# Linear-attention and SwiGLU block: the first chunk's q held in fp32 until its bias is known, and part of the norm sums moved

## The chip, the cores and the metric

The program runs on one core of one Trainium2 chip. The metric is the device time of one execution in microseconds. TensorE multiplies matrices, VectorE and ScalarE work on elements, GpSimd does a few small ones, SyncE (SP) issues the DMAs. [...]

## The reference

All arrays are bf16; x is 2048 rows of 1024.

```python
mod = (silu(c) @ w_mod).reshape(6, 1024)      # sa, ca, ga, sb, cb, gb
h = layernorm(x) * (1 + ca) + sa
q, k, v = split(h @ wqkv)                     # 32 heads of 32
phi = lambda t: where(t > 0, t + 1, exp(t)) + 1e-6
o = phi(q) @ (phi(k).T @ v) / (phi(q) @ sum(phi(k)) + 1e-6)
x = x + ga * (o @ wo)
h = layernorm(x) * (1 + cb) + sb
x = x + gb * ((silu(h @ w_gate) * (h @ w_up)) @ w_down)
```

The change touches the first half alone: the layernorm of x, h, q and k. q of a row needs the shift `sa` only as a constant vector, since (h_scaled + sa) @ wq = h_scaled @ wq + sa @ wq. The kernel uses this for the first 512 rows: it multiplies the scaled rows while `sa` is still being loaded, and adds the bias sa @ wq afterwards.

## The kernel before

**Stages.** The rows are worked in four chunks of 512. For chunk 0, a q phase and then a k phase; for chunks 1 to 3, eight k groups and then eight q groups each (`chunk`, line 837). One group is eight products of a 128x128 weight with 512 rows, accumulated in one PSUM bank over the eight 128-wide pieces of the input (dt 0 to 7). After chunk 3 come the products of phi(k) with the normalised x (`g_group`), the output projection, and the SwiGLU part, which fills the last three quarters of the span.

**Layernorm.** Each of the sixteen 128-row tiles of `XRES` (called x0 to x15 here) gets its sums, on VectorE with BATCH_NORM_STATS (`ln1_stats_ops`) or on ScalarE with two passes that accumulate (`act_stats`, line 574); GpSimd takes the power -0.5; the tile is normalised in place (`ln1_xn`), and SP issues a transposing DMA into `HT` (`th_dma`). `HT` has two halves, for even and odd chunks. There `th_mod` multiplies with 1 + ca and adds sa, per dt. For chunk 0, TensorE transposes instead, and the scaling and the shift are separate (`h0_scale_only`, `h0_shift`).

**q phase of chunk 0** (`q_phase_chunk0`, line 745). Seven groups run side by side in seven banks, two dt at a time, as the weights `wq` arrive. In between stand the products of silu(c) with w_mod for ca and sa (`mod_sc`: 128x128 weights, one column each, into bank 0) and `bias_mm`, 48 products of one column that give the bias into bank 0, columns 16 to 23. The eighth group uses bank 0 after that. Then phi of q is taken from PSUM with the bias (`q_phi`).

**phi** (`phi_evac`, line 654). ScalarE takes exp from the bank into one of four buffers `E1` (for q also relu into `RL`). Of each pair of groups VectorE then takes two TENSOR_SCALAR (min and add) and two final ones (`phi_flush`): for k a SCALAR_TENSOR_TENSOR that reads the bank again, for q a TENSOR_TENSOR of `RL` and `E1`. A k bank is thus free after VectorE's second instruction, a q bank after ScalarE's relu.

**Order.** Every engine runs its instructions in the order in which the program writes them, and a dependency is a semaphore wait; a bank is handed over when the last instruction on it has ended. What stands between the groups is given by dictionaries keyed by the group's number (`kside` for chunk 0's k phase, `s1`, `s2`, `s3` for chunks 1 to 3): the functions of an entry are issued behind that group's products and phi. The bank of a group comes from `next_bank` (line 692): a fixed list of eight, in turn, up to group 40, then five in turn. SP's queue is in order too: loads and transposes that wait for data hold back what is behind them.

**Loads at the start** (lines 397 to 431): x0 to x3, ca, wq, sa, x4 and x5, the first half of wk, x6 and x7, the other half of wk, x8 to x11. The loads of x12 to x15 are issued after chunk 0's q phase (line 830), behind the four transposes of x4 to x7.

**Places of memory that matter.** `WV` (weights of v) and, in the changed kernel, `QPRE` lie at the same 16 KB. `STG` takes 2 MB pieces of w_mod, which VectorE sums with silu(c) (`macc`, eight of 1024 columns for a piece, then `macc_split` and a transpose). `z_row` writes and reads back the sums of phi(k) over SP's queue (`ZB`), `wo_load` brings the output weights, `den` gives the denominators, which go through memory to `RB`.

Of the kernel before, what the change touches and what calls it, by code (L numbers as in the profile page):

```python
# [5 lines left out]
FP32 = mybir.dt.float32  # L6
# [256 lines left out]
def bass_adaLN_cond__linear_attn_block__swiglu_ffn__prompt_kernel(  # L263
# [22 lines left out]
    with ExitStack() as es:  # L286
# [52 lines left out]
        HT = T("ht", 120 * KB, [128, 2, NDT, 512], BF16)  # L339
        WO = T("wo", 120 * KB, [128, NHG, D], BF16)  # L340
# [63 lines left out]
        def sa_load(p):  # L404
            P.dma("wsa%d" % p, WSA[:, :, 512 * p:512 * p + 512], wmv[:, :, 512 * p:512 * p + 512])
# [9 lines left out]
        sa_load(1)  # L415
# [3 lines left out]
        for j in range(2):  # L419
            P.dma("x1_%d" % j, XRES[:, 4 + j, :], xv[:, 4 + j, :])  # L420
        for i in (1, 0):
            P.dma("wk0%d" % i, WQK[:, 4 * i:4 * i + 4, 1024:1536], wqkvv[:, 4 * i:4 * i + 4, 1024:1536])
        for j in range(2, 4):
            P.dma("x1_%d" % j, XRES[:, 4 + j, :], xv[:, 4 + j, :])
# [68 lines left out]
        def th_mod(ch, dt):  # L493
            buf = ch % 2
            if dt % 2 == 0 or ch == 1:
                P.dve("tensor_scalar", out=HT[:, buf, dt, :], in0=HT[:, buf, dt, :], scalar1=MODCOL[:, 0, dt:dt + 1],
                      scalar2=MODCOL[:, 1, dt:dt + 1], op0=ALU.mult, op1=ALU.add)
            else:
                P.act("activation", out=HT[:, buf, dt, :], in_=HT[:, buf, dt, :], func=ACT.Identity,
                      scale=MODCOL[:, 0, dt:dt + 1], bias=MODCOL[:, 1, dt:dt + 1])  # L500
# [23 lines left out]
        def h0_shift(dt):  # L524
            P.dve("tensor_scalar", out=HT[:, 0, dt, :], in0=HT[:, 0, dt, :], scalar1=MODCOL[:, 1, dt:dt + 1],
                  scalar2=None, op0=ALU.add)

        def bias_mm(dts):
            for nt in range(NDT):
                for dt in dts:  # L530
                    P.pe("matmul", out=PS[:, 0, 16 + nt:17 + nt], lhsT=WQK[:, dt, nt * 128:(nt + 1) * 128],
                         rhs=MODTMP[:, dt:dt + 1], start=False, stop=(dt == 3), skip_group_check=True)

        def bias_fin():
            P.dve("tensor_copy", out=BIASQ[:], in_=PS[:, 0, 16:24])
# [17 lines left out]

        def h0_scale(dt):
            P.dve("tensor_scalar", out=HT[:, 0, dt, :], in0=HT[:, 1, dt, :], scalar1=MODCOL[:, 0, dt:dt + 1],
                  scalar2=MODCOL[:, 1, dt:dt + 1], op0=ALU.mult, op1=ALU.add)
# [17 lines left out]
        def act_stats(st, c0=0, mid=None):  # L574
            n = (D - c0) // 512
            junk0 = HT[:, 1, 0:2, :] if st < 8 else JUNK1
# [77 lines left out]
        def phi_evac(bank, dst, bias=0.0):  # L654
            i = phi_ctr[0] % 4
            phi_ctr[0] += 1
            P.act("activation", out=E1[:, i, :], in_=PS[:, bank, :], func=ACT.Exp, bias=bias)
            if not isinstance(dst, tuple):
                P.act("activation", out=RL[:, i, :], in_=PS[:, bank, :], func=ACT.Relu, bias=bias)
            phi_pend.append((i, dst, bank))  # L660
            if len(phi_pend) == 2:
                phi_flush()
# [29 lines left out]
        def next_bank():  # L692
            i = qk_ctr[0]
            qk_ctr[0] += 1
            return (1, 2, 3, 4, 6, 7, 5, 0)[i % 8] if i < 40 else i % 5 + 1

        def q_group(ch, nt):
            buf, bank = ch % 2, next_bank()
            for dt in range(NDT):
                P.pe("matmul", out=PS[:, bank, :], lhsT=WQK[:, dt, nt * 128:(nt + 1) * 128],  # L700
                     rhs=HT[:, buf, dt, :], start=(dt == 0), stop=(dt == NDT - 1))
            phi_evac(bank, PQT[:, nt, ch * 512:(ch + 1) * 512])

        def k_group(ch, nt):
            buf, bank = ch % 2, next_bank()
            for i, dt in enumerate((6, 7, 4, 5, 0, 1, 2, 3) if ch == 0 else range(NDT)):
                P.pe("matmul", out=PS[:, bank, :], lhsT=WQK[:, dt, D + nt * 128:D + (nt + 1) * 128],
                     rhs=HT[:, buf, dt, :], start=(i == 0), stop=(i == 7))
            phi_evac(bank, (ch, nt))
# [35 lines left out]
        def q_phase_chunk0(side):  # L745
# [15 lines left out]
            for nt in range(7):  # L761
                if nt == 4:
                    mod_sc(WSA, 0, range(6, 8))
                    fin_sa(6, 2)
                    for dt in (6, 7):
                        h0_scale(dt)
                q_part(nt, qb[nt], (4, 5))
            mod_sc(WSA, 0, range(4, 6))
            fin_sa(4, 2, True)
            for nt in range(7):  # L770
                if nt == 2:
                    bias_mm((4, 5))
                q_part(nt, qb[nt], (6,))
            for nt in range(7):
                if nt == 1:
                    mod_sc(WSA, 0, range(4))
                    fin_sa(0, 4, True)
                    ln_ops[1][0]()
                    ln_ops[1][1]()
                if nt == 4:  # L780
                    bias_mm(range(4))
                    bias_fin()
                q_part(nt, qb[nt], (7,))
            ln_ops[1][2]()
            ln1_rstd1(5)
# [3 lines left out]
            q_phi = lambda nt: phi_evac(qb[nt] if nt < 7 else 0, PQT[:, nt, 0:512], bias=BIASQ[:, nt:nt + 1])  # L789
            for i, dt in enumerate((4, 5, 0, 1, 2, 3, 6, 7)):  # L790
                P.pe("matmul", out=PS[:, 0, :], lhsT=WQK[:, dt, 896:1024], rhs=HT[:, 0, dt, :], start=(i == 0),
                     stop=(i == 7))
            for dt in (4, 5):
                h0_shift(dt)
            ln1_xn(5)
            th_dma(5)
            for dt in range(4):
                h0_shift(dt)
            ln1_xn(4)
            th_dma(4)  # L800
            for nt in range(8):
                q_phi(nt)
                for f in side.get(nt, []):
                    f()
# [5 lines left out]
        qside, kside = {}, {}  # L810
        ln_ops = [ln1_stats_ops(4 + jj) for jj in range(4)]

        def ln_x1(jj):
            for f in ln_ops[jj]:
                f()
            ln1_rstd1(4 + jj)
        for f in ln_ops[2]:
            add(qside, 1, f)
        for f in ln_ops[3]:
            add(qside, 1, f)  # L820
        add(qside, 1, lambda: ln1_rstd2(6))
        for jj in range(2, 4):
            add(qside, 3, lambda jj=jj: ln1_xn(4 + jj))
            add(qside, 3, lambda jj=jj: th_dma(4 + jj))
# [68 lines left out]
        s3.setdefault(2, []).extend([mod_red, mod_row_a])  # L893
# [321 lines left out]
```

## Time and profile before

| | |
|---|---|
| runs | 828.52, 828.58, 829.11 us (median 828.58) |
| profiled execution | span 827.0 us from the first to the last instruction; the median of the runs is 1.6 us above it |
| TensorE busy | 817.0 us (99%) |
| VectorE, ScalarE busy | 310.8 us (38%), 197.3 us (24%) |
| VectorE busy in 50 to 60, 90 to 100, 120 to 130 us | 9.76, 9.97, 9.86 of 10 |
| chunk 0's k phase begins | 30.41 us |
| chunk 1 begins | 44.21 us |
| last transpose for chunk 1 | landed at 42.97 us |

The span is the time from the first to the last instruction on the chip. A page and a timeline name a group of instructions by line, engine, operation and tile: output tile <- input tiles, shape, count. Nearly all instructions have line 176, a helper's; the tiles tell them apart. In a timeline, the first two columns are start and length in us, and square brackets give the idle time of the engine before the instruction and what ended it. PE is TensorE, PEld its weight loads, DVE VectorE, ACT ScalarE, POOL GpSimd, SPq the DMA queue of SyncE. Matmuls are pipelined: a product of 512 columns lasts 379 ns, and the next one starts 0.216 us after it. Single starts and landings that no view prints are from the trace's records of instructions and semaphores.

### The profile page before, as it was taken

Reading aid. Unit: us, or ns where it says so; the run is one execution under the profiler, and the core shown is the slowest. Engines: PE = TensorE matmul, PEld = TensorE weight load, DVE = VectorE, ACT = ScalarE, POOL = GpSimd, SP = SyncE. Lnnn points to the kernel's source line nnn. Section 1 sums busy time; section 2 is a strip of 40 time slices with the busy share of each in tenths; the row PEclk is TensorE's granted clock in tenths of the full one; section 3 lists DMA queues with packets and bytes.
Section 4 is the critical chain, followed back from the end, with each engine's and each line's share of the span. In section 5 each row is a group of like instructions: output and inputs, shape, how many; then the busy total and the mean of one; then the engine's idle time right before and its main releaser. Section 6 shows DMA issues by size and latency. Waiting matters only on the chain.

```text
span 827.0 us, 10428 instructions
## 1 busy us (share of the span) xinstructions
PE 817.0 (99%) x4244; PEld 376.1 (45%) x4323; DVE 310.8 (38%) x664; ACT 197.3 (24%) x336; POOL 40.7 (5%) x59
## 2 busy tenths in 40 slices
PE   8999999999999999999999999999999999999998
PEld 4544444444444444444444444444444444444444
DVE  5798988476945521111221112122111211221111
ACT  4658643123241111011111101111110111111011
POOL 1010000000130000030000003000000300000000
PEclk9999999999999999999999999999999999999999
DMA  9969665856697995700455570045557004553000
GB/s 317 283 151 225 156 169 144 185 166 200 164 256 234 289 256 153 175 27 23 133 149 152 154 177 29 20 128 153 152 153 185 26 19 124 153 153 87 0 26 26
DMA packets 199360, 119.32 MB, mean 144 GB/s; under 512 B 57992, under 2 KB 183056, under 8 KB 199312
## 3 DMA queue, kind: packets, MB, share of 16 engines
q1 hardware_dynamic: 199296, 118.65, 53.7%
q8 instruction: 34, 0.56, 0.3%
q14 instruction: 14, 0.11, 0.0%
q10 hardware_dynamic: 16, 0.00, 0.0%
HBM read 100.67 MB, written 4.33 MB: 127 GB/s over the span
## 4 chain that ended last, share of the span: by engine, by line
PE 95%; DMA 2%; DVE 1%; SPq 1%; issue 1%; ACT 0%; DVEq 0%; ACTq 0%
PE ps L176 95%; DMA wsa<-in_w_mod_dram 2%; DVE acc L176 1%; SPq L176 1%; DVE pkt L176 0%; DVE e L176 0%; DVE pqt L176 0%; ACT e L176 0%; DVE xres L176 0%; DVE ht L176 0%; DVEq L247 0%; ACTq L247 0%
## 5 line engine op out<-in xcount | busy, mean ns | idle before, releaser
L176 PE MATMUL ps<-h2t,gug 128*128 128x512 bf16 x878 | 210.1, 379 | 0.9
L176 PE MATMUL ps<-h2t,guu 128*128 128x512 bf16 x878 | 209.9, 379 | 0.9
L176 DVE TENSOR_TENSOR at<-sg,ps 128x512 bf16<-128x512 bf16 x112 | 77.0, 688 | 282.7 <-PE ps L176 270.5
L176 ACT ACTIVATE sg<-ps 128x512 bf16<-128x512 f32 x112 | 66.9, 597 | 309.7 <-PE ps L176 298.3
L176 PEld LDWEIGHTS ps<-h2t,guu 128*128 128x128 bf16 x896 | 87.7, 98 | 105.7
L176 PEld LDWEIGHTS ps<-h2t,gug 128*128 128x128 bf16 x896 | 87.6, 98 | 105.5
L176 PE MATMUL ps<-wd_a,at 128*128 128x512 bf16 (+1 forms) x502 | 111.9, 377 | 0.5
L176 PE MATMUL ps<-ht,wqk 128*128 128x512 bf16 x499 | 110.5, 379 | 1.0 <-issue 0.2
L176 PE MATMUL ps<-wd_b,at 128*128 128x512 bf16 (+1 forms) x377 | 84.7, 377 | 0.4
L176 PEld LDWEIGHTS ps<-wd_a,at 128*128 128x128 bf16 x512 | 50.1, 98 | 59.7
L176 DVE TENSOR_TENSOR ut<-att,gb_b 128x512 bf16<-128x512 bf16 (+1 forms) x32 | 13.9, 435 | 167.2 <-ACT att L176 167.2
L176 PEld LDWEIGHTS ps<-ht,wqk 128*128 128x128 bf16 x512 | 49.4, 98 | 59.0 <-DVE ht L176 0.7
L176 ACT ACTIVATE att<-ps 128x512 bf16<-128x512 f32 (+1 forms) x32 | 17.4, 591 | 182.1 <-PE ps L176 182.1
L176 PEld LDWEIGHTS ps<-wd_b,at 128*128 128x128 bf16 x384 | 37.5, 98 | 44.7
L176 PE MATMUL ps<-pk,xres 128*128 128x512 bf16 x250 | 55.4, 379 | 0.6 <-issue 0.5
L176 PE MATMUL ps<-mw,pqt 128*128 128x512 bf16 x249 | 55.5, 379 | 0.5 <-issue 0.2
L176 POOL TENSOR_SCALAR h2t<-h2t,modcol 128x512 bf16<-128x512 bf16 x32 | 26.3, 837 | 383.4 <-DMA h2t<-xn 383.4
L176 ACT ACTIVATE e<-ps 128x512 bf16<-128x512 f32 x56 | 33.2, 604 | 31.9 <-PE ps L176 20.2
L176 PEld LDWEIGHTS ps<-mw,pqt 128*128 128x128 bf16 x256 | 24.7, 98 | 30.2 <-issue 0.5
L176 PEld LDWEIGHTS ps<-pk,xres 128*128 128x128 bf16 x256 | 24.7, 98 | 29.9 <-issue 0.9
L176 ACT ACTIVATE junk<-xres 128x1024 bf16<-128x1024 bf16 x24 | 25.4, 1058 | 34.5 <-DVE xres L176 34.2
L176 DVE SCALAR_TENSOR_TENSOR xres<-ps,xres 128x512 bf16<-128x512 f32 x32 | 21.4, 688 | 11.8 <-PE ps L176 11.6
(107 smaller groups left out, 337.9 us busy)
## 6 DMA issues: line engine op xcount, KB each, us to landing
gug<-in_B_w_gate_dram SPq DMA_DIRECT2D x56, 512.0 KB, 4.0
guu<-in_B_w_up_dram SPq DMA_DIRECT2D x56, 512.0 KB, 5.3
xres<-in_A_x_dram SPq DMA_DIRECT2D x20, 256.0 KB, 4.4
rb<-recip_den SPq DMA_DIRECT2D x8, 512.0 KB, 11.5
stgx<-in_w_mod_dram SPq DMA_DIRECT2D x2, 2048.0 KB, 9.7
wd_a<-in_B_w_down_dram SPq DMA_DIRECT2D x4, 1024.0 KB, 7.4
out_dram<-xres SPq DMA_DIRECT2D x31, 128.0 KB, 1.7
xres<-in_A_x_dram SPq DMA_DIRECT2D x3, 1024.0 KB, 7.1
```

Source lines behind the costliest of these rows:

```text
L176: return getattr(e, method)(**kw)
```

## The change

Chunk 0's q is copied from PSUM as fp32 (`QPRE`) without bias; the shift for chunk 0's k goes into a new tile (`HS`), so the scaled rows stay as they are. The bias products move to chunk 1's q groups: behind each product stands one with the same weights, already in the array, and one column (`bias_mm`, issued without a weight load), into bank 0. phi of chunk 0's q is taken from `QPRE` in the k phases of chunks 2 and 3. The transposes and the norm sums around chunk 0 are ordered anew: x5, x7 and x4 behind the q phase, x6 (sums now on ScalarE) behind the second k group; sums of x8 to x11 in chunk 0's k phase, x12 to x15 earlier in chunk 1. `th_mod` of chunk 1 alternates between VectorE and ScalarE. The loads of x4 to x7 go behind wk's first half, `sa`'s halves change places and go behind wq, the `wv` loads go from chunk 2 to the end of chunk 3, and the sums of w_mod (`macc`) start in chunk 1. `next_bank` has new lists for the first 32 groups.

```diff
+        QPRE = T("qpre", 104 * KB, [128, NHG, 512], FP32)
+        HS = T("hs", 144 * KB, [128, NDT, 512], BF16)
...
         wq_load(4, 2)
-        sa_load(1)
         wq_load(6)
         wq_load(7)
         sa_load(0)
-        for j in range(2):
-            P.dma("x1_%d" % j, XRES[:, 4 + j, :], xv[:, 4 + j, :])
-        for i in (1, 0):
+        sa_load(1)
+        for i in range(2):
             P.dma("wk0%d" % i, WQK[:, 4 * i:4 * i + 4, 1024:1536], wqkvv[:, 4 * i:4 * i + 4, 1024:1536])
-        for j in range(2, 4):
+        for j in range(4):
             P.dma("x1_%d" % j, XRES[:, 4 + j, :], xv[:, 4 + j, :])
...
         def th_mod(ch, dt):
             buf = ch % 2
-            if dt % 2 == 0 or ch == 1:
+            if dt % 2 == 0:
...
+        def bias_mm(nt, dt):
+            w, v, o = WQK[:, dt, nt * 128:(nt + 1) * 128], MODTMP[:, dt:dt + 1], PS[:, 0, nt:nt + 1]
+
+            def fn(e):
+                return e.add_instruction(mybir.InstMatmult(
+                    start_tensor_calc=(nt == 0 and dt == 0), stop_tensor_calc=(dt == NDT - 1), tile_size=(128, 128),
+                    tile_position=(0, 0), ldweights=False, bass_skip_group_check=True,
+                    name=nc.get_next_instruction_name(), ins=[e.lower_ap(v), e.lower_ap(w)], outs=[e.lower_ap(o)]))
+
+            P.add("pe", fn, reads=[w, v], writes=[o], tag="matmul")
...
+            if i < 8:
+                return (2, 3, 4, 6, 7, 5, 0, 3)[i]
+            if i < 24:
+                return (1, 2, 3, 4, 6, 7, 5)[(i - 8) % 7]
+            if i < 32:
+                return (3, 4, 6, 7, 1, 2, 5, 0)[i - 24]
             return (1, 2, 3, 4, 6, 7, 5, 0)[i % 8] if i < 40 else i % 5 + 1
...
+                if ch == 1:
+                    bias_mm(nt, dt)
...
+        def q_copy(nt, bank):
+            P.act("activation", out=QPRE[:, nt, :], in_=PS[:, bank, :], func=ACT.Copy)
...
+            for nt in range(7):
+                q_part(nt, qb[nt], (4, 5))
+            for dt in (6, 7):
+                h0_scale_only(dt)
+            for nt in range(7):
+                q_part(nt, qb[nt], (6,))
+            mod_sc(WSA, 0, range(4))
+            fin_sa(0, 4, True)
+            for dt in range(4):
+                h0_shift(dt)
+            for nt in range(7):
+                q_part(nt, qb[nt], (7,))
+                q_copy(nt, qb[nt])
+            mod_sc(WSA, 0, range(4, 8))
+            fin_sa(4, 4, True)
+            q_part(7, qb[0], range(NDT))
+            q_copy(7, qb[0])
+            for dt in range(4, 8):
+                h0_shift(dt)
             act_stats(4)
+            for j in (5, 7):
+                for f in ln_ops[j - 4]:
+                    f()
+                ln1_rstd1(j)
+            ln1_xn(5)
+            th_dma(5)
             for f in act_mv_ops(4):
                 f()
             neg_rstd(4)
+            ln1_xn(7)
+            th_dma(7)
             ln1_xn(4)
             th_dma(4)
...
+        add(kside, 0, lambda: act_stats(6))
+        for f in act_mv_ops(6):
+            add(kside, 1, f)
+        add(kside, 1, lambda: neg_rstd(6))
+        add(kside, 1, lambda: ln1_xn(6))
+        add(kside, 1, lambda: th_dma(6))
         for dt in range(NDT):
-            add(kside, 1, lambda dt=dt: th_mod(1, dt))
-        for jj, k in ((0, 3), (1, 4)):
-            add(kside, k, lambda jj=jj: act_stats(10 + jj))
-        q_phase_chunk0(qside)
+            add(kside, 4, lambda dt=dt: th_mod(1, dt))
+        for jj in range(2):
+            for f in ln1_stats_ops(8 + jj):
+                add(kside, 5 + jj, f)
+            add(kside, 6 + jj, lambda jj=jj: act_stats(10 + jj))
+        add(kside, 6, lambda: ln1_rstd2(8))
+        q_phase_chunk0()
         for st in range(12, 16):
             x_load(st)
         for gi in range(8):
             k_group(0, gi)
...
-            add(s1, 8 + i, lambda i=i: stg_load(i))
-            add(s2, 1 + i, lambda i=i: wv_load(i))
+            add(s1, 3 + i, lambda i=i: stg_load(i))
+            add(s3, 15, lambda i=i: wv_load(i))
...
+        add(s2, 0, bias_fin)
+        for nt in range(8):
+            add(s2 if nt < 4 else s3, 2 * (nt % 4) + 1, lambda nt=nt: phi_evac(None, PQT[:, nt, 0:512], bias=BIASQ[:, nt:nt + 1],
+                                                       src=QPRE[:, nt, :]))
...
-            add(s2, 4 + kt, lambda kt=kt: macc(STG, kt))
-        add(s2, 13, macc_split)
-        add(s2, 13, lambda: P.dma("stg1", STG[:], wmv[:, :, 4096:5120]))
+            add(s1 if kt < 5 else s2, (11, 12, 13, 14, 15, 8, 9, 10)[kt], lambda kt=kt: macc(STG, kt))
+        add(s2, 11, macc_split)
+        add(s2, 11, lambda: P.dma("stg1", STG[:], wmv[:, :, 4096:5120]))
         for kt in range(NDT):
-            add(s3, 4 + kt, lambda kt=kt: macc(STG, kt))
+            add(s3, 6 + kt, lambda kt=kt: macc(STG, kt))
```

More of the change, by code (lines that the diff above doesn't have):

```diff
@@ L524, in h0_shift @@
         def h0_shift(dt):
[L525 to L532, printed above, removed]
+            if dt < 4:
+                P.dve("tensor_scalar", out=HS[:, dt, :], in0=HT[:, 0, dt, :], scalar1=MODCOL[:, 1, dt:dt + 1],
+                      scalar2=None, op0=ALU.add)
+            else:
+                P.dve("tensor_scalar", out=HS[:, dt, :], in0=HT[:, 1, dt, :], scalar1=MODCOL[:, 0, dt:dt + 1],
+                      scalar2=MODCOL[:, 1, dt:dt + 1], op0=ALU.mult, op1=ALU.add)
+        def bias_mm(nt, dt):
[6 more added lines that the diff above has]
+            P.add("pe", fn, reads=[w, v], writes=[o], tag="matmul")
         def bias_fin():
-            P.dve("tensor_copy", out=BIASQ[:], in_=PS[:, 0, 16:24])
+            P.dve("tensor_copy", out=BIASQ[:], in_=PS[:, 0, 0:8])
         def t_view(dt, n=1):
@@ L552, in raw_copy @@
                 P.dve("tensor_copy", out=dst, in_=src)
-        def h0_scale(dt):
-            P.dve("tensor_scalar", out=HT[:, 0, dt, :], in0=HT[:, 1, dt, :], scalar1=MODCOL[:, 0, dt:dt + 1],
-                  scalar2=MODCOL[:, 1, dt:dt + 1], op0=ALU.mult, op1=ALU.add)
         def ln1_rstd1(st):
@@ L575, in act_stats @@
             n = (D - c0) // 512
-            junk0 = HT[:, 1, 0:2, :] if st < 8 else JUNK1
+            junk0 = HT[:, 1, 0:2, :] if st < 6 else JUNK1
             for fn_, sc_, acc_ in ((ACT.Identity, 1.0 / D, SUMX), (ACT.Square, D ** -0.5, SUMSQ)):
@@ L652, in bass_adaLN_cond__linear_attn_block__swiglu_ffn__prompt_kernel, with phi_evac @@
         phi_ctr = [0]
-        def phi_evac(bank, dst, bias=0.0):
+        def phi_evac(bank, dst, bias=0.0, src=None):
             i = phi_ctr[0] % 4
             phi_ctr[0] += 1
-            P.act("activation", out=E1[:, i, :], in_=PS[:, bank, :], func=ACT.Exp, bias=bias)
+            src = PS[:, bank, :] if src is None else src
+            P.act("activation", out=E1[:, i, :], in_=src, func=ACT.Exp, bias=bias)
             if not isinstance(dst, tuple):
-                P.act("activation", out=RL[:, i, :], in_=PS[:, bank, :], func=ACT.Relu, bias=bias)
+                P.act("activation", out=RL[:, i, :], in_=src, func=ACT.Relu, bias=bias)
             phi_pend.append((i, dst, bank))
@@ L701, in q_group @@
                      rhs=HT[:, buf, dt, :], start=(dt == 0), stop=(dt == NDT - 1))
+                if ch == 1:
+                    bias_mm(nt, dt)
             phi_evac(bank, PQT[:, nt, ch * 512:(ch + 1) * 512])
         def k_group(ch, nt):
-            buf, bank = ch % 2, next_bank()
-            for i, dt in enumerate((6, 7, 4, 5, 0, 1, 2, 3) if ch == 0 else range(NDT)):
+            h, bank = HS if ch == 0 else HT[:, ch % 2], next_bank()
+            for dt in range(NDT):
                 P.pe("matmul", out=PS[:, bank, :], lhsT=WQK[:, dt, D + nt * 128:D + (nt + 1) * 128],
-                     rhs=HT[:, buf, dt, :], start=(i == 0), stop=(i == 7))
+                     rhs=h[:, dt, :], start=(dt == 0), stop=(dt == NDT - 1))
             phi_evac(bank, (ch, nt))
@@ L743, in mod_row_b, with q_phase_chunk0 @@
             P.dma("mdr%d" % i, dst[:], MDR[i].unsqueeze(0).to_broadcast([128, D]))
-        def q_phase_chunk0(side):
+        def q_copy(nt, bank):
+            P.act("activation", out=QPRE[:, nt, :], in_=PS[:, bank, :], func=ACT.Copy)
+        def q_phase_chunk0():
             qb = [1, 2, 3, 4, 6, 7, 5]
@@ L759, in q_phase_chunk0 @@
                 q_part(nt, qb[nt], (2, 3))
-            act_stats(4)
[L761 to L785, printed above, removed]
+            for nt in range(7):
[17 more added lines that the diff above has]
+                h0_shift(dt)
+            act_stats(4)
+            for j in (5, 7):
[4 more added lines that the diff above has]
+            th_dma(5)
             for f in act_mv_ops(4):
@@ L788, in q_phase_chunk0 @@
             neg_rstd(4)
[L789 to L798, printed above, removed]
+            ln1_xn(7)
+            th_dma(7)
             ln1_xn(4)
             th_dma(4)
[L801 to L804, printed above, removed]
             qk_ctr[0] = 0
@@ L808, in add @@
             d.setdefault(k, []).append(f)
-        qside, kside = {}, {}
+        kside = {}
         ln_ops = [ln1_stats_ops(4 + jj) for jj in range(4)]
[L813 to L824, printed above, removed]
-        for dt in range(NDT):
-            add(kside, 1, lambda dt=dt: th_mod(1, dt))
-        for jj, k in ((0, 3), (1, 4)):
-            add(kside, k, lambda jj=jj: act_stats(10 + jj))
-        q_phase_chunk0(qside)
+        add(kside, 0, lambda: act_stats(6))
[4 more added lines that the diff above has]
+        add(kside, 1, lambda: th_dma(6))
+        for dt in range(NDT):
+            add(kside, 4, lambda dt=dt: th_mod(1, dt))
[5 more added lines that the diff above has]
+        q_phase_chunk0()
         for st in range(12, 16):
@@ L870, in ln_half @@
                 add(d, k_fin, lambda jj=jj: neg_rstd(st + 2 + jj))
-        ln_half(2, s1, 0, 0, 1)
+        add(s2, 0, bias_fin)
+        for nt in range(8):
+            add(s2 if nt < 4 else s3, 2 * (nt % 4) + 1, lambda nt=nt: phi_evac(None, PQT[:, nt, 0:512], bias=BIASQ[:, nt:nt + 1],
+                                                       src=QPRE[:, nt, :]))
+        for jj in range(2):
+            for f in act_mv_ops(10 + jj):
+                add(s1, 0, f)
+            add(s1, 0, lambda jj=jj: neg_rstd(10 + jj))
         for jj in range(4):
-            add(s1, 2, lambda jj=jj: ln1_xn(8 + jj))
-            add(s1, 2, lambda jj=jj: th_dma(8 + jj))
+            add(s1, 1, lambda jj=jj: ln1_xn(8 + jj))
+            add(s1, 1, lambda jj=jj: th_dma(8 + jj))
         for i, dt in zip([9, 9, 10, 10, 10, 11, 11, 11], range(NDT)):
             add(s1, i, lambda dt=dt: th_mod(2, dt))
-        ln_half(3, s1, 8, 8, 11)
+        ln_half(3, s1, 6, 6, 9)
         for jj in range(4):
-            add(s1, 13 + jj // 2, lambda jj=jj: ln1_xn(12 + jj))
+            add(s1, 10, lambda jj=jj: ln1_xn(12 + jj))
             add(s2, 0, lambda jj=jj: th_dma(12 + jj))
@@ L892, in bass_adaLN_cond__linear_attn_block__swiglu_ffn__prompt_kernel @@
         add(s1, 7, lambda: P.pool("memset", ap=ZHL[:], constant=0.0))
-        s3.setdefault(2, []).extend([mod_red, mod_row_a])
+        s3.setdefault(0, []).extend([mod_red, mod_row_a])
         add(s3, 12, lambda: mod_row_b(7, 0, GA_B))
```

## The prediction

> Names: k0.0 to k0.7 are the eight k groups of chunk 0 (rows 0-511) in order, k1.0 the first of chunk 1, q7 the last q group of chunk 0; HT1 is chunk 1's half of `HT`; x4 is row tile 4 of `XRES`. Times are us from the start of the span.
>
> **What bounds the kernel now.** First the page.
>
> ```profile
> span 827.0 us, 10428 instructions
> PE 817.0 (99%) x4244; PEld 376.1 (45%) x4323; DVE 310.8 (38%) x664; ACT 197.3 (24%) x336; POOL 40.7 (5%) x59
> L176 PE MATMUL ps<-ht,wqk 128*128 128x512 bf16 x499 | 110.5, 379 | 1.0 <-issue 0.2
> ```
>
> TensorE is busy 99% of the span, and its 499 recorded products of the q/k phases waited 1.0 us in all. So no gain can come from a shorter wait on another engine, and each wait that the change adds is paid in full. Second, TensorE's timeline where the change begins.
>
> ```profile
> 19.77 1.46 PE L176 MATMUL ps<-ht,wqk 128*128 128x512 bf16 x6
> 21.41 0.55 PE L176 MATMUL ps<-siluc,wsa 128*128 128x1 bf16 x16 [0.18 <-DMA wsa<-in_w_mod_dram]
> ...
> 24.04 0.55 PE L176 MATMUL ps<-modtmp,wqk 128*128 128x1 bf16 x16
> ...
> 25.78 0.95 PE L176 MATMUL ps<-siluc,wsa 128*128 128x1 bf16 x32
> ...
> 27.24 0.94 PE L176 MATMUL ps<-modtmp,wqk 128*128 128x1 bf16 x32
> 28.04 3.18 PE L176 MATMUL ps<-ht,wqk 128*128 128x512 bf16 x14
> ```
>
> Six products of 512 columns take 1.46 with a last one of 0.379: one per 0.216. Sixteen of one column take 0.55 with a last one of 0.163: one per 0.025, each with its own weight load hidden in that. Third, the timeline around the start of chunk 1, and the answer for the tile `ht`.
>
> ```profile
> 40.78 1.11 ACT L176 ACTIVATE junk<-xres 128x1024 bf16<-128x1024 bf16 x1
> ...
> 43.10 2.67 DVE L176 TENSOR_SCALAR ht<-ht,modcol 128x512 bf16<-128x512 bf16 x8 [1.54 <-DMA ht<-xres]
> ...
> 45.51 0.10 PEld L176 LDWEIGHTS ps<-ht,wqk 128*128 128x128 bf16 x1 [0.23 <-DVE ht L176]
> ...
> 50.57 1.28 DVE L176 BATCH_NORM_STATS2 stats<-xres 128x6 f32<-128x512 bf16 x2
> ```
>
> ```profile
> L176 SPq DMA_TRANSPOSE ht<-xres x12: 1231/1332/3956, 30.3 to 79.2; - x12
> DMA to landing us min/median/max: 3.2/3.4/7.7
> ```
>
> VectorE waits for the last transpose of rows 512-1023 (landed 42.97), scales HT1 in 2.67 (0.33 each), and TensorE, which began chunk 1 at 44.21, already waits about 0.1 for it at 45.5. This is the place with no slack, and the change rewrites it.
>
> **Part by part.**
>
> *Chunk 0's q phase: -1.7.* Before, k0.0 starts at 28.04 + 11 x 0.2157 = 30.41. After, from the eighth product of dt 4 and 5 (starts 20.84, so the next may start at 21.06): 13 products 2.80, 32 one-column products 0.80, 7 products 1.51, 32 more 0.80, q7's 8 products 1.73: k0.0 starts at 28.70. Gone are 48 bias products (1.2) and waits of 0.5. The cover is the loads. `wsa` part 0 now follows `wq` 6 and 7, so it lands about when those did (22.7, wanted at 23.9); `wsa` part 1 ends the same bytes that ended at 25.73 before (wanted at 26.2); the first `wk` piece then lands near 27.2 (wanted at 28.7), the second near 28.7 (wanted at 29.6). Each would cost its lateness. The eight copies of q to fp32 have the PSUM exponentials as nearest rows (0.48 apart on ScalarE) and lie where ScalarE stood idle (14.7 to 26.4).
>
> *Bias products in chunk 1: +1.6.* 64 products of one column, without a weight load, between products of 512. No row has a product without its load; bounds are nothing and 0.039 (the first of a one-column stream), so 0 to 2.5. I take the 0.025 pitch, 1.6.
>
> *Rows 512-1023 reach HT1 later.* x4 to x7 now load behind both `wk` pieces: 29.4, 30.1, 30.8, 31.5 by the same bytes. VectorE: statistics of x5 and x7 (1.64 each with the small ones, as 53.59 to 55.22 shows) 30.1 to 33.4; normalised x5 at 33.9, x7 34.7, x4 35.5. ScalarE: x4's sums 29.4 to 31.65 (two passes, 2.25 to 2.3 as from 40.78), k0.0's exponential, x6's sums to 34.4, k0.1's exponential to 35.0. VectorE flushes k0.0 and k0.1 (two TENSOR_SCALAR of 0.20, two SCALAR_TENSOR_TENSOR of 0.61: 1.62) to 37.1, and normalises x6 at 38.8. On SP's queue the transposes of x5, x7, x4 stand first; before, the second of these was held until the loads of x8 to x11 had landed (36.85), so the third goes at about 36.9. Then the four loads of x12 to x15 (2.4 at 40.02 before), which this change moves ahead of the last transpose, then x6's, at about 40.4. With 0.7 per 256 KB load (their landings before) it lands behind 2.7 us of loads: L = 44.3. Bounds: 43.0 (3.2 after an issue at 39.8) and 46 (a gap like the 1.5 without traffic at 40 to 41.5 before).
>
> *What queues behind that wait: +8.35.* TensorE is at k1.0 at 28.70 + 64 x 0.2157 = 42.5. The scaling of HT1 now alternates: four on VectorE, four on ScalarE (0.705 apart, from the ACTIVATE ht rows at 65 to 71). They stand on ScalarE ahead of the exponentials of k0.5, k0.6, k0.7. So ScalarE: last scaling done L + 2.9; exponential k0.5 to L + 3.5; k0.6; x10's sums 2.3; k0.7's at L + 6.2 to L + 6.8. VectorE: flush of k0.4 and k0.5 L + 3.55 to L + 5.2; statistics of x8 and x9, now queued here (1.44 + 1.64), to L + 8.25; flush of k0.6 and k0.7 to L + 9.95. The new bank list gives k0.7 bank 3, and k1.2 bank 3 again, three groups later (before: eight). TensorE needs it at 42.5 + 16 x 0.2157 = 45.95 and gets it at L + 10 = 54.3: 8.35 late; 7.05 to 10.05 by the bounds. Inside it lies k1.0 waiting for HT1 (done L + 3.3); from L + 5.0 to L + 10 TensorE does nothing. Afterwards the next used banks have long been drained.
>
> *The clock: +1.5.* At the start of the span thirteen warm-up products of 512 columns from 2.61 to 8.3 stand 0.43 apart, later ones 0.216: after rest TensorE ran at half speed for 5.7. No row shows a gap of 5 us later, so: nothing, or half of 5.7 = 2.9. Neither row is nearer (the start is a longer rest, the later gaps of half a microsecond cost nothing): I take 1.5.
>
> [...]
>
> *Chunks 2 and 3: nothing.* Eight phi of q come here: per group two activations (0.57 with a bias operand at 29 to 34) and 0.54 on VectorE (0.20 + 0.335). VectorE was full at 90 to 100 (9.97 of 10) because of the mod sums (1.2 each); five of eight leave chunk 2, so it has 6.5 (k flushes) + 4.3 (q) + 2.15 (phi) + 3.6 (sums) + 1.8 (their split) + 1.3 (scalings) = 19.7 us of work in 27.6. If that cover failed, TensorE would wait on a bank for the excess.
>
> *The `wv` loads behind chunk 3: +0.3.* They stood in chunk 2; now 2 MB lies on SP's queue ahead of `zb`, `wo` and the denominators. 3.9 us of delay reach `rb`; before, VectorE waited 6.0 for it until 161.6, its eighth G evacuation ended at 163.4, and TensorE wanted that at 167.05: 3.6 of cover. Bounds 0 and 2.4.
>
> **Sum**: -1.7 - 0.1 (the wait at 45.5 goes) + 1.6 + 8.35 + 1.5 + 0.3 = +9.95. It is made on a span of 827.0; the runs' median 828.58 has 1.6 around it, which stays. 828.6 + 9.9 = 838.5.
>
> **Rivals.**
> 1. *Early transposes.* L at 41, with x6's transpose overtaking the loads' data: then k1.2 waits to 51.0, 5.05 late, and with the other terms (-0.2, 1.0 for the clock) the time is 834.4. For it: SP's issues alone would allow 39.7. Against: landings came in order of issue. Chance 0.1.
> 2. *No new wait, the other side.* If VectorE drains bank 3 before 45.95, only -1.8 + 1.6 = -0.2 is left: 828.4. For it: before, a like crowd cost 0.1. Against: even with HT1 landed at 38, VectorE alone (flush to 40.35, four scalings 1.3, flush, 3.1 of statistics, flush) ends at 48.2. Chance 0.07; faster by over 0.2% would need free bias products too, 0.03.
> 3. *The bias products don't come at 0.025.* If each one exposes the next weight load (98 ns), 64 cost 6.3: +4.7, 843.2. Against: the 1-column rows hide a load in 0.025. Chance 0.05.
>
> The forecast has 0.75. Its own range is 833.8 (no clock loss, early bound, free products) to 844.6 (all late bounds together); 8 in 10 of everything lies from 831 to 843.5, which takes in rivals 1 and 3 and leaves out the no-wait case and the joint extreme. Within 0.2% (1.66 us, about what a measurement of this kernel tells from no change) 0.07, faster 0.03, slower 0.90.
>
> **What would show it.** k0.0 near 28.7; the last `ht` transpose of chunk 1 landing 43 to 46; ACTIVATE ht between the fifth and sixth exponential of chunk 0; TensorE idle for some 5 us ahead of the third k group of chunk 1, released by DVE pkt; products 0.43 apart after it; 64 one-column products 25 ns long in the pitch. It is wrong if TensorE shows no gap of over 2 us between 42 and 56.

## The result, and the profile after

| | before | after |
|---|---|---|
| runs, median (from to) | 828.77 us (828.52 to 829.11) | 843.79 us (842.70 to 845.29) |
| ratio, 95% interval | | 1.0185 (1.0172 to 1.0197) |
| profiled execution | span 827.0 | span 841.9, time 843.92 |

The changed kernel is 15.0 us slower. The forecast was 838.5, with a range up to 843.5: right in its sign and in its main mechanism, 5.3 too low. One execution of one experiment (x6's transpose first) took 870.02 us at a granted clock of 0.947 and is left out of its median. The page of the changed kernel:

```profile
span 841.9 us, 10483 instructions
...
PE 825.1 (98%) x4339; PEld 375.2 (45%) x4275; DVE 310.5 (37%) x661; ACT 206.2 (24%) x352; POOL 41.2 (5%) x60
...
L176 PE MATMUL ps<-ht,wqk 128*128 128x512 bf16 x448 | 101.7, 383 | 6.3 <-DVE mv L176 4.6
```

The products of the q/k phases now wait 6.3 us (1.0 before), and their mean length rose from 379 to 383 ns, since eight of them stood 0.427 apart instead of 0.216. Where, the timeline of the start of chunk 1 shows:

```profile
43.82 2.93 ACT L176 ACTIVATE ht<-ht,modcol 128x512 bf16<-128x512 bf16 x4 [5.37 <-DMA ht<-xres]
43.84 1.38 DVE L176 TENSOR_SCALAR ht<-ht,modcol 128x512 bf16<-128x512 bf16 x4 [3.93 <-DMA ht<-xres]
...
44.31 4.61 PE L176 MATMUL ps<-ht,wqk 128*128 128x512 bf16 x16 [1.38 <-DVE ht L176]
...
46.65 1.05 ACT L176 ACTIVATE e<-ps 128x512 bf16<-128x512 f32 x2
...
48.69 1.28 DVE L176 BATCH_NORM_STATS2 stats<-xres 128x6 f32<-128x512 bf16 x2
...
50.13 1.23 DVE L176 BATCH_NORM_STATS2 stats<-xres 128x6 f32<-128x512 bf16 x2
...
52.76 0.68 DVE L176 SCALAR_TENSOR_TENSOR pkt<-ps,e 128x512 bf16<-128x512 f32 x1
...
53.50 0.11 PEld L176 LDWEIGHTS ps<-ht,wqk 128*128 128x128 bf16 x2 [5.08 <-DVE pkt L176]
53.50 4.67 PE L176 MATMUL ps<-ht,wqk 128*128 128x512 bf16 x13 [4.58 <-DVE mv L176]
```

This is the chain of the prediction, in its order: x6's transpose lands (L = 43.71), four scalings on each engine, the exponentials behind them on ScalarE, the norm sums of x8 and x9 on VectorE, then the last read of bank 3 (52.76, ended 53.4), and only then k1.2. The last line's "mv" is a neighbour that ended at the same moment; the line above it names the true releaser. Next, the clock, in stretches of 3 us (the columns are the stretch's length, busy time of PE, PEld, DVE, ACT and POOL, granted clock, DMA share, GB/s):

```profile
50.00:53.00 3.00, 0.00 (x0) 0.00 (x0) 2.93 (x10) 2.97 (x6) 0.70 (x1) 1.00 0.00 0
53.70:56.70 3.00, 3.00 (x8) 1.06 (x7) 2.97 (x13) 0.00 (x0) 1.10 (x2) 0.50 0.86 95
60.00:63.00 3.00, 3.00 (x16) 1.35 (x15) 1.29 (x6) 1.19 (x2) 0.00 (x0) 1.00 1.03 194
180.00:183.00 3.00, 2.83 (x105) 1.65 (x106) 3.00 (x6) 0.72 (x1) 0.00 (x0) 0.50 1.03 217
```

TensorE is idle for the whole first stretch, and the granted clock is then 0.50. The fourth stretch is a second slow one that the prediction did not have, in the stage behind chunk 3 (the G stage). Its timeline:

```profile
139.93 1.67 SPq L176 DMA_TRANSPOSE mhlt<-mhl  x1
...
141.64 4.58 SPq L176 DMA_DIRECT2D wv<-in_A_wqkv_dram  x8
...
146.28 0.32 SPq L176 DMA_DIRECT2D z_row<-zr  x1
...
150.63 0.34 SPq L176 DMA_DIRECT2D zb<-z_row  x1
...
155.28 1.33 ACT L176 ACTIVATE gtmp<-zb,modcol 128x512 f32<-128x512 f32 x2 [17.65 <-DMA zb<-z_row]
...
156.85 20.89 PE L176 MATMUL ps<-pk,xres 128*128 128x512 bf16 x96 [1.07 <-DVE g L176]
...
166.26 4.00 SPq L963 DMA_DIRECT2D rb<-recip_den  x8
...
178.14 1.22 DVE L176 TENSOR_TENSOR pqt<-pqt,rb 128x2048 bf16<-128x2048 bf16 x1 [12.22 <-DMA rb<-recip_den]
...
180.17 0.99 PE L176 MATMUL ps<-g,wv 128*32 128x32 bf16 x100 [2.11 <-DVE g L176]
```

The eight `wv` issues hold SP for 4.6; `z_row` lands at 150.6, 0.2 behind the last `wv` data, and only then is `zb` issued. VectorE waits 12.22 for `rb`, and TensorE now waits for G twice. In the kernel before, where chunk 3 ended 9.0 earlier, the same places were:

```profile
130.14 1.64 SPq L176 DMA_TRANSPOSE mhlt<-mhl  x1
131.84 1.15 SPq L176 DMA_DIRECT2D z_row<-zr  x1
134.56 0.33 SPq L176 DMA_DIRECT2D zb<-z_row  x1
...
149.85 4.00 SPq L955 DMA_DIRECT2D rb<-recip_den  x8
...
161.65 1.23 DVE L176 TENSOR_TENSOR pqt<-pqt,rb 128x2048 bf16<-128x2048 bf16 x1 [5.99 <-DMA rb<-recip_den]
```

**The ledger.** From chunk 0's k phase on, TensorE's weight loads come in the same order in both traces. The start of the same weight load, after less before, tells how late TensorE is there; the steps between places are what each part costs. All in us, one profiled execution each; the columns behind the first belong to experiments told below:

| step | changed kernel | wv early | banks | both | all four | wv alone in the kernel before |
|---|---|---|---|---|---|---|
| up to k0.0 (q phase) | -1.46 | -1.28 | -1.68 | -1.94 | -1.97 | -0.20 |
| wait at k1.0 (HT1) | +1.75 | +3.52 | +2.72 | +2.78 | 0 | 0 |
| k1.0 paced by scalings | +0.67 | +1.13 | +0.67 | +0.67 | +0.27 | +0.08 |
| wait at k1.2 (bank 3) | +4.96 | +4.50 | 0 | 0 | 0 | 0 |
| slow clock behind it | +1.49 | +1.49 | 0 | 0 | 0 | 0 |
| bias products | +1.61 | +1.61 | +1.61 | +1.61 | +1.61 | 0 |
| chunks 2, 3, first G groups | 0 | 0 | 0 | 0 | 0 | 0 |
| G stage to its 13th group | +5.09 | 0 | +5.08 | 0 | 0 | +4.10 |
| from there to the SwiGLU part | +0.79 | +0.86 | +0.86 | 0 | +0.85 | +3.44 |
| span, after less before | +14.9 | +11.8 | +9.3 | +3.1 | +0.8 | +7.5 |

The q phase's row holds 0.25 by which this execution's first product of the phase came later; the part itself is -1.70. A weight load that doesn't wait starts one product (0.2) ahead of its own, so the row of a wait holds 0.2 that the next row gives back: the slow clock behind k1.2 costs 1.69 and shows as 1.49. In the column "wv early" k1.0 costs 0.46 more than in the changed kernel; this execution's mean granted clock was 0.994, against 0.996.

### The profile page after: what moved, and what is told of

It reads as the page before. It is cut to its first block, busy times and chain, and to the rows that moved or that the text cites. A ratio compares the mean times of both kernels' runs of the same rounds, so it can differ in the third digit from the quotient of the medians.

```text
span 841.9 us, 10483 instructions
## 1 busy us (share of the span) xinstructions
PE 825.1 (98%) x4339; PEld 375.2 (45%) x4275; DVE 310.5 (37%) x661; ACT 206.2 (24%) x352; POOL 41.2 (5%) x60
## 3 DMA queue, kind: packets, MB, share of 16 engines
HBM read 100.67 MB, written 4.33 MB: 125 GB/s over the span
## 4 chain that ended last, share of the span: by engine, by line
PE 86%; DMA 5%; DVE 5%; ACT 1%; SPq 1%; issue 1%; POOL 0%; ACTq 0%; DVEq 0%
PE ps L176 86%; DVE acc L176 1%; DMA rb<-recip_den 1%; DMA mhlt<-mhl 1%; DMA recip_den<-rcb 1%; DMA wca<-in_w_mod_dram 1%; ACT ht L176 1%; DVE pkt L176 1%; DMA z_row<-zr 1%; DVE red L176 1%; DVE pqt L176 0%; DMA ht<-xres 0%; SPq L913 0%; DVE mhl L176 0%; SPq L176 0%
## 5 line engine op out<-in xcount | busy, mean ns | idle before, releaser
L176 PE MATMUL ps<-ht,wqk 128*128 128x512 bf16 x448 | 101.7, 383 | 6.3 <-DVE mv L176 4.6
L176 PEld LDWEIGHTS ps<-ht,wqk 128*128 128x128 bf16 x448 | 43.3, 98 | 62.7 <-DVE pkt L176 5.1
L176 PE MATMUL ps<-pk,xres 128*128 128x512 bf16 x256 | 57.5, 384 | 1.1 <-DVE g L176 1.1
L176 ACT ACTIVATE junk<-xres 128x1024 bf16<-128x1024 bf16 x26 | 27.4, 1055 | 35.3 <-DVE xres L176 34.9
L176 DVE SCALAR_TENSOR_TENSOR xres<-ps,xres 128x512 bf16<-128x512 f32 x32 | 21.4, 688 | 11.8 <-PE ps L176 11.6
```

The costliest lines, as they stand in the source:

```text
L176: return getattr(e, method)(**kw)
```

## The experiments

**The `wv` loads back in an earlier place**, chunk 3's q groups:

```diff
-            add(s3, 15, lambda i=i: wv_load(i))
+            add(s3, 8 + i // 2, lambda i=i: wv_load(i))
```

> The eight wv loads go from the end of chunk 3 to behind its first four q groups (two at a time), so they are off SP's queue before the transposes and the small write-and-read of the sums of phi(k). Theory A (the wv loads in front of z_row, wo and rb cost the second stage): the waits of the G stage in the changed kernel (1.24 at its sixth group, 2.28 and 1.62 at the first kvt products and behind them, 5.1 in all) go, zb lands some 4 us earlier, the granted clock stays 1.00 there, and the time falls by 5 to 6, to about 838. Rival B (the stage starts late anyway, because VectorE ends chunk 3 late and its transpose of the w_mod sums holds SP): at most 2 of the 5.1 go, about 842. Neither expects a change before chunk 3.

Measured: 839.09 (838.39 to 840.83), ratio 1.0127 (1.0110 to 1.0144). All waits of the G stage are gone (ledger: 5.09 to 0). This execution's L was 45.65, two later than the changed kernel's, so its span saved less than the stage did.

**Another bank list**, in which bank 3 is not handed from k0.7 to a group three places later:

```diff
-                return (2, 3, 4, 6, 7, 5, 0, 3)[i]
+                return (2, 3, 4, 6, 7, 5, 0, 1)[i]
...
-                return (1, 2, 3, 4, 6, 7, 5)[(i - 8) % 7]
+                return (2, 3, 4, 6, 7, 5, 1)[(i - 8) % 7]
...
-                return (3, 4, 6, 7, 1, 2, 5, 0)[i - 24]
+                return (4, 6, 7, 1, 2, 3, 5, 0)[i - 24]
```

> Only the bank lists of the first 32 groups differ: k0.7 goes to bank 1, and chunk 1 starts with banks 2, 3, 4, 6, 7, 5, 1, so that the bank of k0.7 is wanted again at k1.6 and not at k1.2. Theory A (bank 3 wanted back three groups after k0.7, behind ScalarE's scalings and VectorE's statistics, is the wait): the gap of 4.96 at k1.2 and the slow clock behind it (1.5) go, the wait for the scaled rows at k1.0 (2.4) stays, the time falls by 6 to 6.5, to about 837.5. Rival B (VectorE and ScalarE simply have too much to do there, whatever the list): a gap of several us turns up at a later group of chunk 1, and the time falls by less than 3, to 841 or more.

Measured: 839.05 (838.25 to 840.34), ratio 1.0125 (1.0108 to 1.0142). VectorE's and TensorE's timelines of this kernel:

```profile
53.50 0.68 DVE L176 SCALAR_TENSOR_TENSOR pkt<-ps,e 128x512 bf16<-128x512 f32 x1
```

```profile
45.05 11.30 PE L176 MATMUL ps<-ht,wqk 128*128 128x512 bf16 x46 [2.34 <-DVE ht L176]
```

VectorE is still as late with k0.7's bank (54.2), but TensorE goes through without a wait until 56, the next use of that bank, and its 46 products take 11.30: 1.2 more than 45 steps of 0.216, where eight products 0.427 apart would alone add 1.69. The lateness was harmless by itself; the list turned it into a wait.

**Norm sums of x8 to x11 behind the last k group** of chunk 0, where the flush of k0.6 and k0.7 stands ahead of them:

```diff
-                add(kside, 5 + jj, f)
-            add(kside, 6 + jj, lambda jj=jj: act_stats(10 + jj))
-        add(kside, 6, lambda: ln1_rstd2(8))
+                add(kside, 7, f)
+            add(kside, 7, lambda jj=jj: act_stats(10 + jj))
+        add(kside, 7, lambda: ln1_rstd2(8))
```

> The norm sums of x8 to x11 (two on VectorE, two on ScalarE) move from behind k0.5 to k0.7 to behind k0.7 alone, so that the exponential and the flush of k0.7 come before them. Theory A: bank 3 comes free 2.3 + 3.1 us earlier on the two engines, at best 5 earlier; the gap at k1.2 shrinks from 4.96 to 0 to 2, the clock stays 1.00, the time falls by 4 to 6.5, to 837.5 to 840. Rival B (the scaling of chunk 1's rows on ScalarE alone holds the bank): the gap shrinks by less than 1.5 and the time stays above 842.

Measured: 839.46 (839.05 to 839.61), ratio 1.0128 (1.0111 to 1.0145). TensorE's timeline of this kernel:

```profile
44.68 4.61 PE L176 MATMUL ps<-ht,wqk 128*128 128x512 bf16 x16 [1.94 <-DVE ht L176]
50.83 5.14 PE L176 MATMUL ps<-ht,wqk 128*128 128x512 bf16 x23 [1.54 <-DVE pkt L176]
```

The wait at k1.2 falls from 4.96 to 1.91, and behind this shorter wait 23 products take 5.14, 0.216 apart. So 3.05 of the wait are the moved sums.

**All eight scalings of HT1 on VectorE**, as before the change:

```diff
-            if dt % 2 == 0:
+            if dt % 2 == 0 or ch == 1:
```

> All eight scalings of HT1 on VectorE, as in the kernel before, so that ScalarE doesn't wait for L. Theory A (VectorE's own order, scalings, flush, norm sums of x8 and x9, flush, sets when bank 3 is free): VectorE's chain is L + 2.7 scalings + 1.6 + 3.1 + 1.6 = L + 9.0 instead of the measured L + 9.8; k1.2 waits 0.8 less, 843.0. Theory B (the four scalings on ScalarE, ahead of three exponentials, set it): the wait of 4.96 is gone for the most part, 838 to 839.

Measured: 843.05 (841.89 to 845.18), ratio 1.0178 (1.0159 to 1.0197); within the spread of the changed kernel. The wait at k1.2 is 4.17 (0.79 less), and bank 3 comes at L + 9.15, as VectorE's order gives, instead of L + 9.78. Which engine scales hardly matters; VectorE's order does.

**x6's transpose ahead of the loads of x12 to x15:**

```diff
-        for st in range(12, 16):
-            x_load(st)
         for gi in range(8):
             k_group(0, gi)
...
+            if gi == 1:
+                for st in range(12, 16):
+                    x_load(st)
```

> The loads of x12 to x15 stand behind the transpose of x6 instead of ahead of it. Theory A (the four issues and their traffic make L late): the transpose is issued at 38.3, when x6 has its last scaling, and lands 3.3 to 4.1 later, L = 41.6 to 42.4 instead of 43.7; k1.0 waits 0 to 0.5 instead of 1.75; bank 3 still comes about L + 9.8, near 51.8, so the wait at k1.2 stays near 4.7; whole time some 1.5 to 2 shorter, 842. Theory B (the transposes themselves are slow or stalled, whatever stands ahead): L stays at 43.5 to 44.5 and the time at 843.8.

Measured: 842.3 (841.5 to 842.4), ratio 1.0162 (1.0143 to 1.0181). SP's timeline:

```profile
33.97 5.99 SPq L176 DMA_TRANSPOSE ht<-xres  x4
40.01 2.01 SPq L176 DMA_DIRECT2D xres<-in_A_x_dram  x4
```

The transpose landed 3.06 after its issue: L = 41.79, and TensorE didn't wait at k1.0. With the loads ahead it took 4.14 in the changed kernel (39.57 to 43.71) and 4.57 with the `wv` loads early (41.08 to 45.65). The wait at k1.2 stayed, 4.95. This is the prediction's first rival made on purpose, early transposes, and its 5.05 for that wait.

**Seven eighths of the bias products left out** (chunk 0's q then lacks most of its bias):

```diff
-                if ch == 1:
+                if ch == 1 and nt == 0:
```

> Leaves out seven eighths of the bias of chunk 0's q: 8 of the 64 one-column products of chunk 1 remain. Theory A (each costs 0.028 of TensorE's time and nothing else): chunk 1's q phase is 56 x 0.028 = 1.57 shorter, whole time 842.2. Theory B (they slip into the pipeline of the 512-column products): no change, 843.8. Theory C (each exposes the next weight load of 0.098): 5.5 shorter, 838.3.

Measured: 840.74 (840.40 to 844.02), ratio 1.0156 (1.0140 to 1.0172). In the ledger the row of the bias products falls from 1.61 to 0.20: 1.41 for 56 products, 0.025 each, so theory A with the smaller size. The median fell by 3.0, which the products don't explain; its mean granted clock in three of the four runs was 0.998, against 0.996 in half of the changed kernel's, and 0.002 of 842 us is 1.7, what one stretch of 3.413 at half clock costs.

**Twenty products into a free bank in the wait ahead of k1.2**, so that TensorE isn't idle there:

```diff
         def k_group(ch, nt):
+            if ch == 1 and nt == 2:
+                for _ in range(20):
+                    P.pe("matmul", out=PS[:, 4, :], lhsT=IDENT[:], rhs=HS[:, 0, :], start=True, stop=True)
```

> Twenty products of 512 columns whose result nobody reads go into bank 4 ahead of k1.2 (4.3 us of the gap of 4.96), so TensorE isn't at rest there. Theory A (rest halves the clock): k1.2 starts when it did, 53.5, but its eight products stand 0.216 apart and not 0.427, the granted clock stays 1.00 from 50 to 60, and the time falls by 1.5 to 1.7, to about 842.2. Rival B (the slow products come from something else, such as a contended bank): they stay 0.427 apart and the time stays the same.

Measured: 846.96 (843.98 to 848.48), ratio 1.0214 (1.0190 to 1.0239): a miss in the whole, a hit in its place. k1.2 started as late as ever (53.51), and its products then stood 0.216 apart and not 0.427: 1.69 saved. But the G stage cost more, with a wait of 2.38 that no tile explains (2.21 <-issue in its row), and slow products behind it (16 in 5.23 at 185.97, against 3.63). The granted clock of the three longer runs was 0.996, 0.994 and 0.994, that of the profiled one 0.998: by an estimate from 3.413 at half clock, one to two slow stretches of 1.7 more, at places that no trace shows. The next two runs are about the wait.

**The same with the `wv` loads early** (the first and the last edit together).

> 20 products that write to a free bank stand in the wait ahead of k1.2, as in an earlier run, now with the wv loads in chunk 3, where the G stage has no waits. Theory A (they only keep the clock up, and the higher time of the earlier run came from the G stage): 839.1 less 1.5 to 1.7 of slow clock, 837.5. Theory B (the products themselves cost time, wherever): 841 or more.

Measured: 838.82 (838.18 to 839.24), ratio 1.0123 (1.0108 to 1.0138): between the two theories, 0.3 under early `wv` loads alone. The first products recorded behind the wait ahead of k1.2 stand 0.22 apart (5 in 1.25, from 54.93). TensorE's timeline in the G stage:

```profile
180.93 0.43 PE L176 MATMUL ps<-wo,kvt 32*32 32x512 bf16 x15
182.39 0.37 PE L176 MATMUL ps<-wo,kvt 32*32 32x512 bf16 x1 [1.03 <-issue]
```

A wait of 1.03 that no tile explains ("issue"). The twenty products alone have one of 2.21 in this stage, the `wv` loads alone in the kernel before one of 1.69. The page has a queue of instruction packets, 34 with 0.56 MB in the span. The wait ended 2.6 after one of 16 KB began, as the expectation of the next run has it; whose instructions a packet holds, no row tells.

**One weight load for the twenty products**, which makes TensorE's program 19 instructions shorter (`warm_mm` issues a product without a weight load, as `bias_mm` does):

```diff
-                for _ in range(20):
-                    P.pe("matmul", out=PS[:, 4, :], lhsT=IDENT[:], rhs=HS[:, 0, :], start=True, stop=True)
+                P.pe("matmul", out=PS[:, 4, :], lhsT=IDENT[:], rhs=HS[:, 0, :], start=True, stop=True)
+                for _ in range(19):
+                    warm_mm(IDENT[:], HS[:, 0, :], PS[:, 4, :])
```

> As the run with 20 products in the wait and the early wv loads, but the 20 products use one weight load, so TensorE's program is 19 instructions shorter. In that run TensorE stood 1.2 in the G stage, between two products that waited for nothing, from 1.2 after the start of a 16 KB instruction fetch to 2.6 after it; the fetch began 0.5 ahead of the last piece of rb. Theory A (the fetch is held behind rb's pieces, and TensorE ran out of instructions because the added ones had moved the place in its program at which it has to fetch): with 19 fewer, about 2 us more work lies ahead of that place, the stall is gone, the fetch still begins 0.4 to 0.9 ahead of the last rb piece, and the time is 1.2 less, 837.6. Theory B (the stall has nothing to do with the number of instructions): it stays at 1.2, 838.8.

Measured: 836.87 (836.83 to 838.72), ratio 1.0103 (1.0087 to 1.0120), 1.95 less, of which the wait explains some 1.2. The same place in this kernel:

```profile
181.61 0.43 PE L176 MATMUL ps<-wo,kvt 32*32 32x512 bf16 x16
181.98 3.63 PE L176 MATMUL ps<-pk,xres 128*128 128x512 bf16 x16
```

No wait: with 19 instructions fewer, some 130 us ahead of this place, it is gone, as theory A expected. That TensorE ran out of instructions, and that a packet was held behind `rb`'s data, is the author's explanation and was not shown. Among the timelines of this stage, the wait stands in those of three programs that have 32 or 40 more weight loads and products ahead of it than the changed kernel; the kernel before, with 32 more, has none over 0.16. Nor has this one, with 21 more, or the changed kernel.

**The `wv` loads at the end of chunk 3, alone, in the kernel before:**

```diff
-            add(s2, 1 + i, lambda i=i: wv_load(i))
+            add(s3, 15, lambda i=i: wv_load(i))
```

> The kernel before with one part of the change alone: the wv loads at the end of chunk 3. The prediction's account of this part gives +0.3, at most +2.4: 828.8 to 830.9. Theory A (the part was mis-sized by itself: the sums of phi(k) land behind the data of wv and zb 5.9 later, rb 6.5 later, of which 3.6 are covered, and a slow clock may follow): +3 to +4.3, 831.6 to 832.9. Theory B (the account is right for this part alone, and the 5.1 of the changed kernel come from its meeting with the moved sums of w_mod): 829.5 or less.

Measured: 834.66 (833.92 to 836.20), ratio 1.0076 (1.0061 to 1.0091), +6.4: over the upper end of theory A, and far from theory B. SP's timeline of this kernel:

```profile
130.02 1.63 SPq L176 DMA_TRANSPOSE mhlt<-mhl  x1
131.70 4.63 SPq L176 DMA_DIRECT2D wv<-in_A_wqkv_dram  x8
136.39 0.46 SPq L176 DMA_DIRECT2D z_row<-zr  x1
141.18 0.34 SPq L176 DMA_DIRECT2D zb<-z_row  x1
141.55 4.22 SPq L905 DMA_DIRECT2D wo<-in_A_wo_dram  x8
145.82 3.05 SPq L176 DMA_DIRECT2D recip_den<-rcb  x4
155.92 4.02 SPq L955 DMA_DIRECT2D rb<-recip_den  x8
```

Against the kernel before, `z_row` is issued 4.55 later (131.84), `zb` 6.62 (134.56), `rb` 6.07 (149.85). The waits are 4.1, and in this execution a wait of 1.85 that no tile explains (1.69 <-issue in its row) and a slow clock (1.6; the mean granted clock was 0.998) came on top.

**The sums of w_mod in chunk 3 two groups earlier**, as they were:

```diff
-            add(s3, 6 + kt, lambda kt=kt: macc(STG, kt))
+            add(s3, 4 + kt, lambda kt=kt: macc(STG, kt))
```

> The changed kernel with the w_mod sums of chunk 3 back behind groups 4 to 11 (they stand behind 6 to 13). Theory A (the later sums hold the transpose of mhl back by 0.8 at the end of chunk 3, and the wv loads stand behind it): the G stage waits some 0.8 less, 843.0. Theory B (the wv loads alone set it): 843.8, the G stage's waits 5.1.

Measured: 843.23 (842.26 to 844.08), ratio 1.0179 (1.0162 to 1.0196). The transpose of `mhl` goes 2.53 behind the first G group instead of 3.86, and the G stage costs 3.73 instead of 5.09; in the whole time 0.6, too little to tell from the spread. A small share, on theory A's side.

**Bank list and early `wv` loads together.**

> The bank list and the place of the wv loads are changed together. If the bank wait at k1.2 with the clock behind it (5 to 5.6) and the waits of the G stage (5.1) are two separate costs, both go: 843.8 - 5.0 - 5.1 = 833.7, 832.8 to 834.5. If one is only the other shifted (the cover in the G stage shrinks when chunk 1 ends early, or the other way), less than 8 goes: 836 or more.

Measured: 832.85 (832.10 to 834.62), ratio 1.0055 (1.0042 to 1.0069). The two costs are separate, and both go.

**Those two, the late norm sums and x6's transpose first: all four together.**

> Bank list, early wv loads, norm sums of rows 1024-1535 late, x6's transpose ahead of the loads of x12 to x15. By the theory of four separate waits what is left against the kernel before is: q phase -1.7, HT1 0 to 1 at k1.0 and 0.5 to 0.7 in its scaling, 64 one-column products +1.8, and up to 0.8 at 236 to 241: +0.6 to +2.6, so 829.4 to 831.4, 830.5 the likeliest. A rival by which a cost was missed (the fp32 copies, or phi of q in chunks 2 and 3) leaves it at 832 or more. Faster than the kernel before would need the one-column products hidden.

Measured: 830.21 (829.51 to 831.22, 11 runs; the kernel before 828.52), ratio 1.0020 (1.0012 to 1.0029). The page's line for the products of the q/k phases:

```profile
L176 PE MATMUL ps<-ht,wqk 128*128 128x512 bf16 x448 | 99.4, 379 | 0.1
```

They wait 0.1 us in all, and up to the 13th G group TensorE is 0.07 ahead of the kernel before: the q phase's gain, eaten by the bias products. The runs are still 1.7 us longer than the kernel before; this execution shows 0.85 of that near 225 (see "What was not foreseen besides"). So the idea of the change, repaired, comes to nothing, and no run pointed to a version that beats the kernel before.

## Why the prediction was wrong, step by step

**The step that failed** is the term "the `wv` loads behind chunk 3: +0.3, bounds 0 and 2.4", in its sentence "3.9 us of delay reach `rb`; [...] 3.6 of cover". Measured against the end of chunk 3, `rb` was issued 7.4 later, and the term is 5.1 (removed by the first experiment, 4.1 to 7.5 by itself in the kernel before). Three things were left out. The prediction counted the time in which SP issues (3.9; measured 4.6), but `z_row`'s own data waits behind the 2 MB too (4.3 from issue to landing, 2.7 before), and a chain of round trips follows: `zb`, `rb`. The sums of w_mod, moved behind two more groups, delayed the transpose ahead of the loads (0.8 against before; with them back it went 1.3 earlier). And only the cover of `rb` was counted: `zb`'s lateness has a wait of its own (1.24 net), and behind `rb`'s (2.23) come a second slow stretch (1.1) and a wait for VectorE's copy of `kvt`, which is multiplied with `wo` (0.5). Had 7.4 stood in the prediction's own account, 7.4 less 1.24 less 3.6 = 2.6 would have been the `rb` wait, near the measured 2.23: the cover held, the delay put against it didn't.

**What held.** The q phase: -1.70 for -1.7. The bias products: 1.61 for 1.6, and the rival of 0.098 each fell (seven eighths removed: 0.20). HT1: L = 43.71 for 44.3, bounds 43.0 and 46; over the traces with the predicted queue order it ran from 43.7 to 45.7. Bank 3: seven traces with the changed order have it at L + 9.78 or 9.79, for L + 10; the wait in all 1.75 + 0.67 + 4.96 = 7.4 for 8.35, the difference mostly L. The mechanism is shown three times: another list removes it, the sums' place is 3.05 of it, the scalings' engine 0.79. Chunks 2 and 3: 0 for 0. The clock: 1.49 in the ledger for 1.5, which is luck in its size, since the 1.5 was the middle between nothing and 2.9. It comes of eight products 0.427 apart instead of 0.216, 1.69 in all, which the runs with the twenty products gave back.

In the changed kernel's trace the granted clock is 0.50 from 53.63 to 57.05 and from 179.93 to 183.34, 3.413 each, and 1.00 for 47.79 ahead of the first drop and for 122.88 between the two, which are 14 and 36 times 3.413. The second drop came behind a gap of 2.11, the first behind one of 5.08. In the run with the bank list a gap of 2.34 had no such cost behind it, so in these runs it is not the length of the gap alone that tells. The stretches of 3.413 that end at the two drops are those in which TensorE was busy least, from the first full clock (5.85) to 260 us: 0.04 of the first, 0.45 of the second. The next two (43.39 to 46.81 and 46.81 to 50.22), busy for 0.64 and 0.62, had full clock behind them. In the kernel before, where no stretch up to 260 us was busy for less than 0.91, the clock was 1.00 from 8.31 to the end of the span. What sets the clock was not tried further than that.

**What was not foreseen besides.** 0.8 near 238: a transpose of `mhl` (the split sums of w_mod) took 5.85 instead of 4.32, one of its parts landing 1.7 behind the first, and VectorE, then TensorE, waited for it. In the ledger four columns with the change have 0.79 to 0.86 of it and one has none, with the same instructions around it. What lengthened the transpose is not shown: an instruction packet begins inside it (236.51), but one also begins inside the changed kernel's transpose of `mhl` at 105.80, which took 4.33, and none inside the one at 278.18 in the kernel before, which took 5.81. Besides, 0.25 of a later start, and 2.0 instead of 1.6 around the span. The sum: 4.8 (`wv`) - 0.95 (bank 3) + 0.8 + 0.25 + 0.4 = 5.3, which is what the forecast missed.

## What to carry to other kernels

A bulk load moved on an in-order queue costs what stands behind it (in the kernel before, 4.6 of issues made `zb` 6.62 late): follow every small round trip behind it to its landing, not to its issue, and ask at each landing, not only the last, who waits and with what cover. A bank or buffer list is a due time: when work is moved in front of the instruction that frees a buffer, count the groups until the list comes to that buffer again. And when a change is repaired until nothing waits, what is left (here 64 products at 0.025 against 48 and half a microsecond of waits) is what the idea was worth.

## What the runs showed of the hardware

- In the changed kernel the granted clock was 0.50 for 3.413 us behind gaps of TensorE of 5.08 and 2.11; in the 3.413 ahead of each drop TensorE was busy for 0.04 and 0.45. Behind 3.413 busy for 0.62 and 0.64 it stayed at 1.00, and behind a gap of 2.34 in another run 46 products took 11.30, too little for eight at half pace.
- A one-column product that uses the weights already in the array cost 0.025 between products of 512 columns (64 cost 1.61). In the kernel before, 16 with a weight load of their own took 0.55 in a stream, 0.025 apart.
- In three traces TensorE waited 1.03, 1.69 and 2.21 us in the G stage for nothing that a row names; with 19 instructions fewer, far ahead, the wait of 1.03 was not there. What it waited for is not shown.
- x6's transpose landed 3.06 after its issue with no load ahead of it on its queue, and 4.14 and 4.57 behind four 256 KB loads in two other traces.
- A transpose of `mhl` landed 4.25 to 5.81 after its issue in the kernel before (four of them), and 4.32 to 6.28 in the changed kernel.
